# Ninety-one tiny loads as marks in a decode kernel that runs at the DMA engines' rate

## The chip, the cores and the metric

One core of a Trainium2 chip. The metric is device microseconds of one execution. SP, ACT and POOL below are the three engines that issue loads (SyncE, ScalarE, GpSimd); PE and DVE are the matmul and vector engines. "Landed" means that all of a load's semaphore increments have come. Each DMA engine has its own ring of work; a load "in the rings" has been issued and not yet moved. A mark is one of the tiny loads that the change adds, a series is fifteen of them, K8 is the K load of unit 8, and a drain is a stretch in which the rings hold no large load.

## The reference

One decode step of attention with a cached K and V, in sum with a gated MLP on the same normalised input:

```python
B, Sq, D = (4, 1, 640); H, Sk, Dh = (32, 4096, 128)
def _A_ref(x, k_cache, v_cache, wq, wo):
    q = (x @ wq).reshape(B, Sq, H, Dh)...            # cut
    scores = jnp.einsum('bhqd,bhkd->bhqk', q, k_cache) * Dh ** (-0.5)
    p = _softmax(scores, axis=-1)
    o = jnp.einsum('bhqk,bhkd->bhqd', p, v_cache)
    return (o ...) @ wo                              # cut
return x + _A_ref(xn, ...) + _B_ref(xn, ...)         # _B_ref: gMLP, weights of 3.3 MB in all
```

K and V together are 268 MB in bfloat16; every byte is read once.

## The kernel before

It cuts K and V into sixteen units each (8 heads of one batch entry, 8.4 MB) and streams them through five slots of one SBUF buffer. All large loads go over SP's queue, one unit ahead of the unit that is being worked on. The parts that the change touches:

```python
wq = at_slot(0, n_q)...; nc.sync.dma_start(out=wq, in_=A_wq...)          # 5.2 MB
nc.sync.dma_start(out=w_in, in_=B_w_in...)                               # 2.2 MB
nc.sync.dma_start(out=w_out, in_=B_w_out[0:nf, :]...)                    # 0.8 MB
for r in range(4):
    nc.sync.dma_start(out=w_rest[r:32:4], in_=w_rest_d[r])               # L125, 8 rows each
# ... cut: the order of units (k0 k1 k2 k3 v0 k4 v1 k5 ...) and their slots
def load_unit(item):
    # ... cut
    for t0, t1 in zip(c[:-1], c[1:]):
        nc.sync.dma_start(out=unit(item, t0, t1), in_=src[:, t0 * Dh:t1 * Dh])   # L161
def load_wo(g, c_cuts=(0, HG)):
    for c0, c1 in zip(c_cuts[:-1], c_cuts[1:]):
        nc.sync.dma_start(out=wo_t[g][:, c0:c1, :], in_=wo_q[g][:, c0:c1, :])    # L169
load_unit(seq[0])
# ... cut: constants on GpSimd, layer norm, q, the MLP
for i, item in enumerate(seq):
    if i + 1 < len(seq):
        key, u = seq[i + 1]
        # ... cut: x_res, the residual, 2 x 2.5 KB, ahead of the last V load but one
        load_unit(seq[i + 1])
        if key == "k" and u == 2 * B - 1:
            load_wo(u // B - 1)
    else:
        load_wo(NG - 3); load_wo(NG - 2); load_wo(NG - 1, (0, 4, 6, 7, 8))
    # ... cut: work on `item`
```

The framework that builds the program places every semaphore wait.

Of the kernel before, what the change touches and what calls it, by code (L numbers as in the profile page):

```python
# [12 lines left out]
BF16 = mybir.dt.bfloat16  # L13
# [3 lines left out]
def kernel(  # L17
# [19 lines left out]
    nc = tc.nc  # L37
    P = 128
    B, Sq, D = A_x.shape
# [27 lines left out]
    const = ctx.enter_context(tc.tile_pool(name="const", bufs=1))  # L67
# [78 lines left out]
    def unit(item, t0, t1):  # L146

        s0, s1 = place[item]
        assert s1 == s0 + 1 or t1 <= T // 2 or t0 >= T // 2
        if t0 >= T // 2:  # L150
            return at_slot(s1, (t1 - t0) * Dh, t0 * Dh - SL)
        return at_slot(s0, (t1 - t0) * Dh, t0 * Dh)

    def load_unit(item):
        key, u = item
        g, b = divmod(u, B)
        cache = A_k_cache if key == "k" else A_v_cache
        src = cache[b, g * HG:(g + 1) * HG].rearrange("e (m t) d -> (e m) (t d)", t=T)
        c = cuts.get(item, (0, T))
        for t0, t1 in zip(c[:-1], c[1:]):  # L160
            nc.sync.dma_start(out=unit(item, t0, t1), in_=src[:, t0 * Dh:t1 * Dh])  # L161
# [5 lines left out]
    def load_wo(g, c_cuts=(0, HG)):  # L167
        for c0, c1 in zip(c_cuts[:-1], c_cuts[1:]):
            nc.sync.dma_start(out=wo_t[g][:, c0:c1, :], in_=wo_q[g][:, c0:c1, :])  # L169

    load_unit(seq[0])


# [79 lines left out]
    MkH = SelH[:G]  # L253
    B32 = const.tile([G, B], BF16)
    nc.gpsimd.tensor_copy(out=B32[:], in_=Mk4[:G])

    NW = T // 4
    Zb = []
# [91 lines left out]
    def fill_qz(g):  # L350
        for hp in range(HP):
            r0 = 32 * hp
            nc.gpsimd.tensor_copy(out=QZ[r0:r0 + 32, :, :, :, 8 + 8 * hp],  # L353
                                  in_=qT[32 * g:32 * g + 32, NE * hp:NE * hp + NE].rearrange("p e a b -> p b a e"))
# [4 lines left out]
    def emit_K(u, k):  # L359

        g, b = divmod(u, B)
        hh = first.get(u, 0) ^ (k // 4)
        qp, kh = k // 2 % 2, k % 2
        t0 = 2 * TC * (2 * hh + qp)
        kw = unit(("k", u), t0, t0 + 2 * TC).bitcast(F32).rearrange("p (t w) -> p t w", w=KW)[:, :, 32 * kh:32 * kh + 32]
        kT = ktpool.tile([P, NKT], F32, tag="kT", name="kT")[:, 0:2 * TC * 32]
        nc.vector.transpose(kT[:].rearrange("p (t r) -> p t r", r=32), kw)  # L367
        if ("S", g) not in state:
            S_new = ps_s.tile([P, NE, TC, M], F32, tag="S", name="S")
            state[("S", g)] = S_new  # L370
        S_ps = state[("S", g)]
        kb = kT[:].bitcast(BF16).rearrange("p (i t e m w) -> p i t e m w", i=2, e=NE, m=M, w=2)
        w0 = 8 - (b * C2 + hh)
        for w in range(2):
            for e in range(NE):
                for i in range(2):
                    q = 2 * qp + i
                    nc.tensor.matmul(S_ps[32 * q:32 * q + 32, e], lhsT=QZ[:, b, 2 * kh + w, e, w0:w0 + 32],  # L378
                                     rhs=kb[:, i, :, e, :, w], start=(b == 0 and k < 4 and kh == 0 and w == 0),
                                     stop=(b == B - 1 and k >= 4 and kh == 1 and w == 1))  # L380
# [34 lines left out]
    def softmax(g):  # L415
        negmax = softmax_max(g)
        S_ps = state.pop(("S", g))
        p_bf = ppool.tile([P, TC, NE, M], BF16, tag="p", name="p")
        rowsum = small.tile([P, NE], F32, tag="rowsum")
        for e in range(NE):  # L420
            nc.scalar.activation(out=p_bf[:, :, e, :], in_=S_ps[:, e], func=ACT.Exp, bias=negmax[:, e:e + 1], scale=scale,  # L421
                                 accum_out=rowsum[:, e:e + 1])

        pT = ppool.tile([P, TC, HP, B * C2], BF16, tag="p", name="pT")
        nc.vector.transpose(pT[:].rearrange("p t h x -> p (t h x)"), p_bf[:].rearrange("p t e m -> p (t e m)"))  # L425

        xd = small.tile([P, B * C2, 4, TC], BF16, tag="xd", name="xd", bufs=1)
        state[("xd", g)] = xd
        for hp in range(HP):
            for q in range(4):  # L430
                op = nc.vector.tensor_copy if q < 2 or (hp < 3 and q == 2) else nc.scalar.copy
                op(out=xd[32 * hp:32 * hp + 32, :, q, :], in_=pT[32 * q:32 * q + 32, :, hp, :].rearrange("p t x -> p x t"))  # L432
        z_fill(g, 0)
        z_fill(g, 1)
        cs = misc_ps([G, 1], F32)
        for e in range(NE):
            nc.tensor.matmul(cs[:], lhsT=SelPe[:, e].rearrange("p h e b -> p (h e b)"), rhs=rowsum[:, e:e + 1],  # L437
                             start=(e == 0), stop=(e == NE - 1))
        rinv = small.tile([G, 1], F32, tag="rinv")
        nc.vector.reciprocal(out=rinv[:], in_=cs[:])  # L440
        state[("rinv", g)] = rinv
# [26 lines left out]
    def emit_sel(g):  # L468

        oh = misc_ps([G, Dh], F32)  # L470
        for b in range(B):
            nc.tensor.matmul(oh[:], lhsT=SelR[:, b].rearrange("p h b -> p (h b)"), rhs=state["R"][:, b, :],  # L472
                             start=(b == 0), stop=(b == B - 1))
        om = ppool.tile([G, HG, Dh], BF16, tag="p", name="om")
        nc.vector.scalar_tensor_tensor(out=om[:], in0=oh[:, None, :].to_broadcast((G, HG, Dh)),  # L475
                                       scalar=state.pop(("rinv", g))[:, 0:1],
                                       in1=MkH[:, :, None].to_broadcast((G, HG, Dh)), op0=ALU.mult, op1=ALU.mult)
        state[("om", g)] = om

    def emit_oT(g):  # L480
        om = state.pop(("om", g))[:].rearrange("p h (q c) -> p c h q", c=HG)
        oT_ps = misc_ps([P, HG, B], F32)
        for c in range(HG):
            nc.tensor.matmul(oT_ps[:, c, :], lhsT=om[:, c, :, :], rhs=B32[:], start=True, stop=True)
        oT = small.tile([P, HG + 1, B], BF16, tag="oT", bufs=3)
        nc.vector.tensor_copy(out=oT[:, 0:HG, :], in_=oT_ps[:])
        if g == NG - 1:
            nc.gpsimd.memset(oT[:, HG, :], 0.0)
        state[("oT", g)] = oT

    def emit_proj(g, cs=range(HG)):
        oT = state[("oT", g)]
        for c in cs:
            for hf in range(NH):
                r0 = 64 * (c % 2) + 32 * hf
                nc.tensor.matmul(proj[r0:r0 + B, 0:NO2], lhsT=oT[:, c, :],
                                 rhs=wo_t[g][:, c, hf * NO2:(hf + 1) * NO2],
                                 start=False, stop=(g == NG - 2 and c >= HG - 2))

    fill_qz(0)  # L500
# [3 lines that stand above are left out]
            if u == NU - 2 and key == "v":  # L504
                for hf in range(NH):
                    nc.sync.dma_start(out=x_res[32 * hf:32 * hf + B, :], in_=x_flat[:, hf * NO2:(hf + 1) * NO2])
            load_unit(seq[i + 1])
            if key == "k" and u == 2 * B - 1:
                load_wo(u // B - 1)
        else:  # L510
            load_wo(NG - 3)
            load_wo(NG - 2)
            load_wo(NG - 1, (0, 4, 6, 7, 8))
        key, u = item
        g, b = divmod(u, B)
        if key == "k":
            done = b == B - 1 and g > 0
            for k in range(8):
                emit_K(u, k)
                if done and k == 1:  # L520
                    emit_sel(g - 1)
                if done and k == 2:
                    emit_oT(g - 1)
                if done and k == 5 and g == 1:
                    emit_proj(g - 1)
            if b == B - 1:
                if g < NG - 1:
                    fill_qz(g + 1)
                softmax(g)
        else:  # L530
            emit_V(u)
# [59 lines left out]
```

## Time and profile before

| | before |
|---|---|
| median time | 664.23 us (2 runs, 664.21 to 664.24) |
| span in the profile | 662.5 us |
| bytes over the DMA engines | 282.61 MB, 427 GB/s on average |
| busiest compute engine | DVE, 54% |

How to read it: the compute engines have slack, the DMA engines have none. The prediction shows the lines; its first part explains them.

### The profile page before, as it was taken

The page shows a single profiled execution, that of the slowest core. Times are in us where ns is not written, and L with a number is a line of the kernel's source. Part 1 is how long each engine was busy: PE and PEld are TensorE (multiplying, and loading weights), DVE is VectorE, ACT ScalarE, POOL GpSimd, SP SyncE. Part 2 cuts the span into 40 slices and gives each one's busy share as a digit, 9 for nine tenths or more (in the row PEclk, how much of TensorE's full clock was granted, in tenths as well). Part 3 has the DMA queues.
Part 4 walks back from the last instruction along what each step waited for, and adds up shares of the span by engine and source line. Part 5 has one row for each costly group of instructions (what it writes and reads, how often), then busy time and mean ns, then how long its engine had stood idle before and what let it go on. Part 6 is the DMA issues. An engine that isn't in the chain of part 4 may idle for free.

```text
span 662.5 us, 5421 instructions
## 1 busy us (share of the span) xinstructions
PE 292.9 (44%) x2297; PEld 106.5 (16%) x2297; DVE 360.1 (54%) x275; ACT 78.4 (12%) x162; POOL 20.3 (3%) x64
## 2 busy tenths in 40 slices
PE   0636666256072556225336054533506254623245
PEld 0111122112021122111112022111202112211122
DVE  2249899556191759618256286745619185951112
ACT  0300000530100000530200000071010000053200
POOL 6210000000000000000000000000000000000000
PEclk9858768678577587677859596756958759667767
DMA  9999999999999999999999999999999999999996
GB/s 371 463 424 427 426 444 437 435 436 416 443 432 423 439 418 442 433 439 440 423 420 435 432 421 452 433 424 431 431 436 444 428 431 415 445 432 437 418 419 262
DMA packets 6901, 282.61 MB, mean 427 GB/s; under 512 B 808, under 2 KB 1084, under 8 KB 1468
## 3 DMA queue, kind: packets, MB, share of 16 engines
q1 hardware_dynamic: 6856, 282.25, 98.8%
q8 instruction: 18, 0.29, 0.2%
q14 instruction: 7, 0.06, 0.0%
q10 hardware_dynamic: 20, 0.01, 0.0%
HBM read 282.25 MB, written 0.01 MB: 426 GB/s over the span
## 4 chain that ended last, share of the span: by engine, by line
DMA 74%; DVE 11%; issue 11%; PE 2%; ACT 1%; SPq 0%; DVEq 0%; ACTq 0%
DMA kv<-in_A_k_cache_dram 64%; DVE kT L367 11%; DMA kv<-in_A_v_cache_dram 5%; DMA kv<-in_A_wo_dram 3%; DMA kv<-in_A_wq_dram 2%; PE O L449 2%; ACT xd L432 0%; ACT Zb L413 0%; ACT p L421 0%; DVE pT L425 0%; PE last_a L553 0%; DVE m L385 0%; PE S L378 0%; SPq L169 0%; PE misc L390 0%
## 5 line engine op out<-in xcount | busy, mean ns | idle before, releaser
L367 DVE STREAM_TRANSPOSE kT<-kv 128x2048 f32<-128x2048 f32 x128 | 282.8, 2276 | 124.7 <-DMA kv<-in_A_k_cache_dram 124.7
L378 PE MATMUL S<-kT,QZ 128*32 128x512 bf16 x1024 | 187.9, 500 | 230.6 <-DVE kT L367 230.6
L378 PEld LDWEIGHTS <-QZ 128*32 128x32 bf16 x1024 | 60.3, 111 | 353.4 <-issue 332.6
L449 PE MATMUL O<-kv,Zb 128*32 128x512 bf16 x1024 | 73.6, 451 | 58.2 <-DMA kv<-in_A_v_cache_dram 38.0
L458 DVE TENSOR_TENSOR om<-O,Mk 128x512 f32<-128x512 f32 x15 | 10.4, 692 | 109.0 <-PE O L449 109.0
L413 ACT ACTIVATE Zb<-xd,MkE 32x256 bf16<-32x256 bf16 x116 | 52.9, 498 | 110.4 <-PE O L449 109.0
L421 ACT ACTIVATE p<-S,negmax 128x512 bf16<-128x512 f32 x8 | 5.4, 683 | 400.6 <-DVE negmax L399 400.6
L449 PEld LDWEIGHTS <-Zb 128*32 128x32 bf16 x1024 | 32.9, 112 | 97.4 <-issue 55.8
L472 PE MATMUL misc<-R,SelR 128*32 128x128 f32 x32 | 6.4, 281 | 30.0 <-DVE R L459 28.4
L353 POOL COPY QZ<-qT 32x32 bf16<-32x32 bf16 x16 | 5.1, 318 | 390.6 <-PE S L378 389.9
L432 DVE COPY xd<-pT 32x256 bf16<-32x256 bf16 x44 | 16.0, 365 | 0.8
L459 DVE TENSOR_REDUCE R<-om 128x128 f32<-128x512 f32 x15 | 15.3, 1019 | 0.5
L432 ACT COPY xd<-pT 32x256 bf16<-32x256 bf16 x20 | 12.3, 614 | 5.6 <-DVE pT L425 5.2
L425 DVE STREAM_TRANSPOSE pT<-p 128x1024 bf16<-128x1024 bf16 x4 | 5.0, 1245 | 6.3 <-ACT p L421 6.3
L472 PEld LDWEIGHTS misc<-R,SelR 128*32 128x32 f32 x32 | 2.2, 107 | 37.8 <-DVE R L459 26.0
L385 DVE TENSOR_REDUCE m<-S 128x2 f32<-128x1024 f32 x4 | 4.9, 1225 | 5.5 <-PE S L378 5.5
L274 PE MATMUL q<-kv,xnT 128*32 128x512 bf16 x40 | 4.5, 630 | 6.9 <-DMA kv<-in_A_wq_dram 6.9
L461 DVE TENSOR_SCALAR R<-O,Mk 128x128 f32<-128x128 f32 x1 | 0.4, 351 | 12.5 <-PE O L449 12.5
L282 DVE CAST kv<-q 128x512 bf16<-128x512 f32 x1 | 0.7, 692 | 11.1 <-PE q L274 11.1
L390 PE MATMUL misc<-dg,ones_f 128*128 128x256 f32 x8 | 3.2, 488 | 7.6 <-DVE dg L387 7.6
L475 DVE SCALAR_TENSOR_TENSOR om<-misc,rinv,SelH 32x1024 bf16<-32x1024 f32 x4 | 5.1, 1271 | 2.0 <-PE misc L472 2.0
L437 PE MATMUL misc<-rowsum,SelPe 128*32 128x1 f32 x16 | 2.1, 202 | 9.0 <-ACT p L421 9.0
(102 smaller groups left out, 78.2 us busy)
## 6 DMA issues: line engine op xcount, KB each, us to landing
kv<-in_A_k_cache_dram SPq DMA_DIRECT2D x8, 4096.0 KB
kv<-in_A_v_cache_dram SPq DMA_DIRECT2D x1, 6144.0 KB
kv<-in_A_wq_dram SPq DMA_DIRECT2D x1, 5120.0 KB
kv<-in_A_wo_dram SPq DMA_DIRECT2D x3, 1280.0 KB
kv<-in_B_w_in_dram SPq DMA_DIRECT2D x1, 2160.0 KB, 19.9
kv<-in_A_v_cache_dram SPq DMA_DIRECT2D x1, 2048.0 KB
kv<-in_B_w_out_dram SPq DMA_DIRECT2D x1, 800.0 KB
kv<-in_A_wo_dram SPq DMA_DIRECT2D x1, 640.0 KB, 22.0
```

Of the source, the lines that this page charges most:

```text
L353: nc.gpsimd.tensor_copy(out=QZ[r0:r0 + 32, :, :, :, 8 + 8 * hp], in_=qT[32 * g:32 * g + 32, NE * hp:NE * hp + NE].rearrange("p e a b -> p ...
L367: nc.vector.transpose(kT[:].rearrange("p (t r) -> p t r", r=32), kw)
L378: nc.tensor.matmul(S_ps[32 * q:32 * q + 32, e], lhsT=QZ[:, b, 2 * kh + w, e, w0:w0 + 32], rhs=kb[:, i, :, e, :, w], start=(b == 0 and k < ...
L413: nc.scalar.activation(out=dst, in_=src, func=ACT.Copy, scale=mk)
L421: nc.scalar.activation(out=p_bf[:, :, e, :], in_=S_ps[:, e], func=ACT.Exp, bias=negmax[:, e:e + 1], scale=scale, accum_out=rowsum[:, e:e + 1])
L425: nc.vector.transpose(pT[:].rearrange("p t h x -> p (t h x)"), p_bf[:].rearrange("p t e m -> p (t e m)"))
L432: op(out=xd[32 * hp:32 * hp + 32, :, q, :], in_=pT[32 * q:32 * q + 32, :, hp, :].rearrange("p t x -> p x t"))
L449: nc.tensor.matmul(O_ps[32 * q:32 * q + 32, :, :], lhsT=Zb[b % 2][:, w].rearrange("p h c -> p (h c)"), rhs=vv[:, w * 4 * Dh:(w + 1) * 4 * ...
L458: nc.vector.tensor_tensor(out=om4[:], in0=O_ps[:], in1=Mk4[:, :, None].to_broadcast((P, 4, Dh)), op=ALU.mult)
L459: nc.vector.tensor_reduce(out=R, in_=om4[:].rearrange("p c d -> p d c"), axis=AX.X, op=ALU.add)
L472: nc.tensor.matmul(oh[:], lhsT=SelR[:, b].rearrange("p h b -> p (h b)"), rhs=state["R"][:, b, :], start=(b == 0), stop=(b == B - 1))
L475: nc.vector.scalar_tensor_tensor(out=om[:], in0=oh[:, None, :].to_broadcast((G, HG, Dh)), scalar=state.pop(("rinv", g))[:, 0:1], in1=MkH[: ...
```

## The change

Its intent is a tool for reading traces: loads of 1, 2, ... 15 rows are meant to run on as many DMA engines, so that their packets would show where each engine stands at five moments of the run. Nothing reads what they load.

```diff
+    mk = const.tile([16, 4, 136], BF16)
+    mk_ctr = [0]
+    def marks():
+        for k in range(1, 16):
+            nc.sync.dma_start(out=mk[0:k, mk_ctr[0] % 4, :], in_=A_wo[16 * k:17 * k, 0:136])
+            mk_ctr[0] += 1
+    marks()
     load_unit(seq[0])
@@ among the constants on GpSimd
+    mk2 = const.tile([1, 16, 64], BF16)
+    for k in range(16):
+        nc.gpsimd.dma_start(out=mk2[:, k, 0:31 + 2 * k], in_=A_wo[k:k + 1, 0:31 + 2 * k])
@@ main loop
             load_unit(seq[i + 1])
+            if key == "k" and u in (B, 2 * B, 3 * B):
+                marks()
             if key == "k" and u == 2 * B - 1:
                 load_wo(u // B - 1)
         else:
+            marks()
             load_wo(NG - 3)
```

## The prediction

> **What bounds the kernel now.** I read the page's busy shares first, then its slices, then the waits of the SP queue, then the chain that ended last, then single stretches of the timeline.
>
> ```profile
> span 662.5 us, 5421 instructions
> PE 292.9 (44%) x2297; PEld 106.5 (16%) x2297; DVE 360.1 (54%) x275; ACT 78.4 (12%) x162; POOL 20.3 (3%) x64
> ...
> DMA  9999999999999999999999999999999999999996
> ...
> DMA packets 6901, 282.61 MB, mean 427 GB/s; under 512 B 808, under 2 KB 1084, under 8 KB 1468
> ...
> DMA 74%; DVE 11%; issue 11%; PE 2%; ACT 1%; SPq 0%; DVEq 0%; ACTq 0%
> ```
>
> No compute engine passes 54%; the DMA digit is 9 in 39 of 40 slices and the chain is 74% DMA. The table of stretches shows the same at a finer grain: a DMA share of 1.00 and 430 to 433 GB/s from 24 to 650 us. So this kernel's time is its bytes over its rate, 282.6 MB at 427 GB/s = 662 us, and it holds only because the ring never runs dry. Any microsecond in which the slowest DMA engine has nothing queued is added to the end; nothing later can win it back.
>
> How far ahead is the queue filled? The timeline of SP and the chain around the K load that is unit 8 (the load after which the change puts its third series):
>
> ```profile
> 266.59 0.33 SPq L161 DMA_DIRECT2D kv<-in_A_k_cache_dram  x1
> 285.94 0.33 SPq L161 DMA_DIRECT2D kv<-in_A_v_cache_dram  x1
> 308.73 0.33 SPq L161 DMA_DIRECT2D kv<-in_A_k_cache_dram  x1
> ```
> ```profile
> 266.59 33.20 DMA kv<-in_A_k_cache_dram
> ```
>
> K8 is issued at 266.59 and has landed at 299.79. The V load behind it is issued at 285.94, 13.9 us before that, so it stands in the rings when K8 ends. SP itself is nearly always waiting, never working:
>
> ```profile
> SPq L161 <- DMA kv<-in_A_k_cache_dram: 182.1, 15, 19.6
> SPq L161 <- DVE kT L367: 155.9, 17, 16.8
> ...
> SPq L125 <- DMA kv<-in_A_wq_dram: 11.5, 1, 11.5
> ...
> SPq L586 <- DMA out_dram<-o_bf: 1.1, 1, 1.1
> ```
>
> The third line is the one to see. L125 loads the rest of w_out into its own buffer and shares no byte with wq, yet SP stood 11.5 us until wq had landed. The built program says why: loads of the hardware queues take eight semaphores in turn, and a load waits until the one eight before it, on its semaphore, has landed. It also shows waits of a load for an earlier load into the same bytes (K2, over K0's slot, waits for K0's semaphore as well as for K0's readers).
>
> **What the Trainium skill says.** "DMA: Bandwidth & Descriptors", section "Queues, rings and completion order": each DMA engine takes the descriptors of one ring in order. So a tiny load behind an 8 MB load on SP's queue lands only when that engine has done its share. The trace agrees: x_res, 2.5 KB, was issued at 581.33 and its four increments came between 607.58 and 610.72, beside the 606.25 to 610.62 of the V load ahead of it. The same page, "Why a DMA increments its semaphore by 16 and not by 1": a load of few rows runs on the lowest k engines, and one slow engine of the four came last here (610.72), so the slowest engine sits among the first four; a mark of 4 or more rows waits for it. "Perfetto Trace Analysis", section "DMA Instruction — HWDGE (DVE, Sync)": the profiled window of an issue leaves out the movement, so the 0.33 us above is SP's cost, not the load's. The DMA page's "Latency and other measured facts" has about 0.6 us to the first byte; here it was more: x issued at 0.73 has its first packet at 1.69, and the output issued at 660.00 at 0.82 us later. I use 0.9.
>
> **The change part by part.** Nothing is removed. In bytes it is nothing: 5 x 120 rows x 272 B = 163 KB and 16 rows of under 130 B, 0.4 us at 427 GB/s. In descriptors, 15 marks put at most 15 x 2 packets on one engine; a packet of 640 B took about 32 ns, so under 1 us on an engine in a series.
>
> The waits are the cost. The buffer has four slots and mark j+4 writes rows that mark j writes, so it waits for mark j to have landed, unread though it is; beyond this mark 8 waits for the load just ahead of the series (eight before it). SP is in order, so the next big load stands behind mark 15. For the series after K8:
>
> 1. Marks 1 to 4 are issued at once behind K8 and lie in the rings until K8's share on their engines is done, about 299.4 on the slowest engine.
> 2. Mark 1 lands 0.5 us later (own packet, its increment; increments follow their 4-byte packet by 0.35 to 0.45 us in this trace). SP has stood for 32 us by then, and the V load that had been issued at 285.94 has not been.
> 3. Marks 5 to 15 go out, eleven issues. By issue cost: x_res shows 0.37 us from one tiny issue to the next, the small wo pieces at the end 0.47; eleven are 4.1 to 5.2 us. By latency: a tiny load on an idle queue takes about 1.5 us from issue to landing (the output: 1.1 us of waiting after 0.4 us), so 5 to 8, 9 to 12 and 13 to 15 are two full rounds and three issues, 2 x 1.55 + 3 x 0.4 = 4.3. Both act together; I take 4.8.
> 4. The V load is issued and its first packet comes 0.9 us on.
>
> Sum: 0.5 + 4.8 + 0.9 = 6.2 us in which the slowest engine has nothing but marks. The faster engines end K8 up to 3.7 us earlier (its increments span 296.07 to 299.79) and idle longer, which costs nothing. Series 2 (after K4) and 4 (after K12) have the same form; K4's V load was issued only 7 us before K4 landed, but that is still ahead of it. So 3 x 6.2 = 18.6.
>
> The first series stands behind wq, w_in, w_out and the four w_rest loads and ahead of K0. In the kernel before, K0 is issued at 16.60, and the increments of the last w_rest come at 23.28 to 23.72, from where K0 flows. With marks, mark 3 waits for w_in (21.03), mark 4 for w_out (22.93), marks 5 to 8 for w_rest and for marks 1 to 4 (about 23.7): the rings empty, then the same eleven issues. K0 is issued at about 28.6 and flows from 29.5, 5.8 us late.
>
> The fifth stands behind the last V load, whose increments end at 649.67, and ahead of the six wo issues, which were all out at 637.2. They go out from 655 on; 9.7 us of wo and the same last products and output follow. 6.2 us.
>
> The sixteen loads on GpSimd's queue: POOL is done with its constants at about 14.6 and waits until 23.12 for the transposed q:
>
> ```profile
> 13.74 0.73 POOL L302 MEMSET kv<- 128x768 f32 x1
> 14.42 0.20 POOL L307 MEMSET one_bf<- 1x128 bf16 x1
> 23.12 0.29 POOL L285 COPY qT<-kv 128x128 bf16<-128x128 bf16 x1 [8.50 <-DVE kv L283]
> ```
>
> Each load costs POOL perhaps 1 us (the skill's figure for that path's start; no such load is in this trace), and the ninth may wait for the first. Some 16 to 20 us would bring q's copy from 23 to 31 to 35. What waits for it: the K1 load (needed in the ring when K0 ends, then about 49) and the query weights for the first product (needed at about 51). Hidden, 0 us.
>
> Sum: 5.8 + 18.6 + 6.2 = 30.6, less about 0.6 where series reset the engines' spread (all restart together): 30. Predicted 664.2 + 30 = 694.
>
> **The rivals.**
> - *Marks are only bytes.* If the waits for the four slots were not made, or the marks were sent ahead of the big loads, the change costs 0.4 to 2 us: 665 to 666. For it: the trace of before has spare time on SP (it waits 13.9 us ahead of need). Against it: the eight semaphores in turn alone make mark 8 wait for the load ahead of it and leave eight issues after that: 8 x 0.4 + 0.4 + 0.9 = 4.5 us a series, 687 in all. Also against: SP's order in the trace follows the program, even for x_res, which nothing held back.
> - *The first marks land on fast engines.* If marks 1 to 3 go to engines that end early, marks 5 to 7 are out before K8 is done and only mark 8 waits for all of it. Then eight issues remain, 4.5 us a series, 687. I give it a fifth.
> - *Issues on few engines are dear.* The w_rest loads of 8 rows took 0.62 us to issue, alone on the queue too (15.94). If marks cost this, eleven are 7.2 us and a series 8.6: 707.
> - *GpSimd becomes the bound.* If each of its loads cost 2.5 us or more, q's copy would come after 54, K1 would come late and the rings run dry once more, up to 10 us on top. The depth of 15 us speaks against.
> - *DVE or PE take over.* A series stops loads but no compute; DVE at 54% falls to about 52%. No.
>
> **Range and chances.** The issue cost (0.37 to 0.62) and whether mark 1 waits for the slowest engine set the spread: 687 at one end, 703 for somewhat dearer rounds (2.2 us of latency gives 7.1 a series, 698, and 0.5 us per issue adds to it). I say 686 to 703. Slower by over 2% means over 677.5; it takes 13.3 us, under half of the sum, so 0.95; within 2% 0.045.
>
> **What would show each step.** Right: five dips in the DMA row and in GB/s, near 24 to 30, 146, 311, 473 and past 660, each 5 to 7 us, GB/s outside them unchanged at 430 to 433; a stand of SP of some 30 us at the marks' line, waiting for a K load or for mk; in the timeline the V load that came 13.9 us before K8's end now about 5 us after it; wo issued after the last V has landed. POOL's copy of q after 30 with K1 still issued before K0 ends. Wrong: the V loads issued before the K load has landed (then no wait for slots), dips of 10 us (dearer issues), a sixth gap after K0 (GpSimd), or a lower rate between the dips, which none of these steps explains.

## The result, and the profile after

The changed kernel takes 671.81 us (2 runs, 671.29 to 672.32). The ratio to before is 1.0115, with a 95% interval of 1.0096 to 1.0134. (A ratio here and below is taken over the fast runs of the same rounds, so it isn't quite the ratio of the medians.) It is 7.6 us slower, where 30 had been predicted.

First the page of the changed kernel: its span, the GB/s of the 40 slices, the sum of DMA packets, and the chain by engine.

```profile
span 670.5 us, 5523 instructions
...
GB/s 373 381 428 423 411 434 444 434 435 428 439 435 422 430 417 456 415 431 431 434 436 431 431 412 453 438 435 438 412 439 423 431 430 423 442 431 434 433 403 192
DMA packets 8613, 282.78 MB, mean 422 GB/s; under 512 B 2520, under 2 KB 2796, under 8 KB 3180
...
DMA 76%; DVE 11%; issue 11%; PE 1%; SPq 1%; DVEq 0%
```

The bytes are up by 0.17 MB, as worked out (163 KB). But the GB/s row has none of the five dips that were predicted. There is a low second slice (381) and a low end (403, 192), and between them the rate of before. So the middle three series drained nothing. The timeline of SP around K8, whose times stand beside the three lines of before in the prediction, shows why (start us, duration us, engine, line, what; L176 is the marks' line):

```profile
269.88 0.33 SPq L161 DMA_DIRECT2D kv<-in_A_k_cache_dram  x1
270.27 1.18 SPq L176 DMA_DIRECT2D mk<-in_A_wo_dram  x4
289.25 0.35 SPq L161 DMA_DIRECT2D kv<-in_A_v_cache_dram  x1
301.90 1.88 SPq L176 DMA_DIRECT2D mk<-in_A_wo_dram  x4
312.10 0.35 SPq L161 DMA_DIRECT2D kv<-in_A_k_cache_dram  x1
322.74 1.41 SPq L176 DMA_DIRECT2D mk<-in_A_wo_dram  x4
326.26 0.35 SPq L161 DMA_DIRECT2D kv<-in_A_v_cache_dram  x1
```

The fifteen marks are not one block. After four of them comes the V load, at 289.25, which is 19.4 us after K8's issue, just as before (285.94 less 266.59). Marks 5 to 8 wait for marks 1 to 4 and are issued at 301.90, when the V load has long been in the rings. The order of SP's instructions in the two built programs says the same; this is the excerpt around K8, with the rows between marks 1 and 4 and so on cut:

```
 K load 128x32768
+mk 1x136 ... mk 4x136
 V load 128x32768
+mk 5x136 ... mk 8x136
 K load 128x32768
+mk 9x136 ... mk 12x136
 V load 128x32768
+mk 13x136 ... mk 15x136
```

The source says fifteen marks, then the V load. The builder laid down one big load after each four marks.

Where, then, do 7.6 us come from? From the two places where an interleaved load doesn't help. The start, SP's queue after and then before:

```profile
17.01 6.74 SPq L176 DMA_DIRECT2D mk<-in_A_wo_dram  x4
23.79 0.36 SPq L161 DMA_DIRECT2D kv<-in_A_k_cache_dram  x1
24.27 1.49 SPq L176 DMA_DIRECT2D mk<-in_A_wo_dram  x4
26.25 0.35 SPq L161 DMA_DIRECT2D kv<-in_A_k_cache_dram  x1
```
```profile
16.60 7.16 SPq L161 DMA_DIRECT2D kv<-in_A_k_cache_dram  x2
```

K0 is issued at 23.79 instead of 16.60. The stretches 20 to 26 and 26 to 32 us, before and after (the last two columns are the DMA share and GB/s):

```profile
20.00:26.00 6.00, 5.35 (x29) 1.07 (x24) 1.94 (x2) 0.69 (x2) 1.57 (x5) 1.00 1.22 520
26.00:32.00 6.00, 1.23 (x4) 0.59 (x3) 1.75 (x6) 4.35 (x6) 1.41 (x3) 0.68 0.98 426
```
```profile
20.00:26.00 6.00, 5.45 (x33) 1.20 (x25) 1.94 (x2) 0.59 (x1) 5.25 (x10) 1.00 1.02 349
26.00:32.00 6.00, 1.54 (x5) 0.59 (x3) 1.75 (x6) 4.14 (x6) 2.55 (x8) 0.66 0.81 350
```

(520 is more than sixteen engines do in steady flow, 433 at 27.1 GB/s each: packets are counted where they start.) Over these 12 us the rate is 350 instead of 473 GB/s, 1.48 MB less; at 427 GB/s that is 3.5 us.

And the end, before and then the changed kernel; before, all six wo loads went out from 631.59 to 637.2:

```profile
631.59 5.64 SPq L169 DMA_DIRECT2D kv<-in_A_wo_dram  x6
```
```profile
621.20 1.18 SPq L176 DMA_DIRECT2D mk<-in_A_wo_dram  x4
635.92 0.35 SPq L169 DMA_DIRECT2D kv<-in_A_wo_dram  x1
652.63 2.53 SPq L176 DMA_DIRECT2D mk<-in_A_wo_dram  x4
655.21 0.35 SPq L169 DMA_DIRECT2D kv<-in_A_wo_dram  x1
656.99 1.41 SPq L176 DMA_DIRECT2D mk<-in_A_wo_dram  x4
658.44 0.35 SPq L169 DMA_DIRECT2D kv<-in_A_wo_dram  x1
660.96 1.15 SPq L176 DMA_DIRECT2D mk<-in_A_wo_dram  x3
662.14 2.17 SPq L169 DMA_DIRECT2D kv<-in_A_wo_dram  x3
```

Here the load that slips ahead is a wo load of 1.3 MB, 3.1 us of DMA time (1.31 MB over 427 GB/s), and not a V load of 19.6 us. Each group of four marks waits for the group before, so the rings are fed one wo load at a time. The chain of the changed kernel runs through the marks at this point:

```profile
621.20 31.41 DMA mk<-in_A_wo_dram
...
652.63 4.34 DMA mk<-in_A_wo_dram
...
656.99 3.95 DMA mk<-in_A_wo_dram
```

### The profile page after: what moved, and what is told of

Same layout as the page of the kernel before. It is cut to its first block, busy times and chain, and to the rows that moved or that the text cites. A ratio compares the mean times of both kernels' runs of the same rounds, so it can differ in the third digit from the quotient of the medians.

```text
span 670.5 us, 5523 instructions
## 1 busy us (share of the span) xinstructions
PE 296.8 (44%) x2297; PEld 107.6 (16%) x2297; DVE 360.0 (54%) x275; ACT 78.4 (12%) x162; POOL 28.6 (4%) x80
## 4 chain that ended last, share of the span: by engine, by line
DMA 76%; DVE 11%; issue 11%; PE 1%; SPq 1%; DVEq 0%
DMA kv<-in_A_k_cache_dram 62%; DVE kT L380 11%; DMA mk<-in_A_wo_dram 6%; DMA kv<-in_A_v_cache_dram 4%; DMA kv<-in_B_w_out_dram 3%; PE O L462 1%; DMA kv<-in_A_wo_dram 0%; SPq L169 0%; SPq L176 0%; SPq L161 0%; DVE o_bf L576 0%; PE last_a L569 0%; DVEq L380 0%; SPq L113 0%; SPq L110 0%
## 5 line engine op out<-in xcount | busy, mean ns | idle before, releaser
L462 PE MATMUL O<-kv,Zb 128*32 128x512 bf16 x1024 | 76.1, 463 | 58.9 <-DMA kv<-in_A_v_cache_dram 38.8
L268 POOL DMA_DIRECT2D mk<-in_A_wo_dram x16 | 8.5, 537 | 3.7 <-DMA mk<-in_A_wo_dram 3.6
```

Source lines behind the costliest of these rows:

```text
L268: nc.gpsimd.dma_start(out=mk2[:, k, 0:31 + 2 * k], in_=A_wo[k:k + 1, 0:31 + 2 * k])
L462: nc.tensor.matmul(O_ps[32 * q:32 * q + 32, :, :], lhsT=Zb[b % 2][:, w].rearrange("p h c -> p (h c)"), rhs=vv[:, w * 4 * Dh:(w + 1) * 4 * ...
```

## The experiments

Twelve kernels ran, all correct, each with five rounds against the kernel before (the record of `e_in_order` holds four of its runs). The theory after the result (A): the builder interleaves the loads, so a series costs its packets only, except at the start, where marks and K0 wait for loads that are the last in the rings, and at the end, where the interleaved loads are short. Rivals: (B) the packets of the marks cost the same wherever they stand; (C) GpSimd's loads make the start late.

### One part at a time

`a_first`, `b_middle`, `c_last` keep one group of series and drop GpSimd's loads; `d_gpsimd` keeps those alone.

```diff
-    marks()                                            # dropped in b, c, d
-            if key == "k" and u in (B, 2 * B, 3 * B):  # dropped in a, c, d
-                marks()
-            marks()                                    # ahead of load_wo: dropped in a, b, d
-    for k in range(16):                                # GpSimd: dropped in a, b, c
+    for k in range(0):
```

> The first series of fifteen marks alone, no GpSimd loads. Theory A (the places count: K0 is issued at 23.8 instead of 16.6, after the rings have run empty): 3.5 to 4 us over before, near 668. Theory B (each mark costs its packets wherever it stands, 7.6 us over five series): 1.5 us, near 665.8. Theory C (the GpSimd loads make the start late): under 1 us, near 665.

> The three series in the middle alone. Theory A (the scheduler lets a K or V load go ahead after every four marks, so the rings never run dry): 0.3 to 1.2 us over before in all, 664.5 to 665.4. Theory B (packets, three fifths of 7.6): 4.5 us, near 668.8. The step of my prediction (three drains of 6.2): 683.

> The last series alone. Theory A (wo loads two to six stand behind marks that wait for the last V load, and only four marks and one wo load are in the rings at a time): 3 to 4 us over before, 667.2 to 668.2. Theory B: 1.5 us, 665.8. My prediction's step: 6.2 us, 670.4.

> The sixteen GpSimd loads alone. Theory A: 0 to 0.5 us over before, up to 664.7 (q's copy on POOL moves from 23.1 to about 26, K1 is still ahead of need). Theory C (they slow the start): 3 us or more, over 667.

| kernel | median us (5 runs) | over before (664.14, same rounds) | ratio, 95% interval |
|---|---|---|---|
| first series | 667.61 | 3.47 | 1.0054, 1.0041 to 1.0066 |
| three middle series | 665.03 | 0.89 | 1.0013, 1.0001 to 1.0026 |
| last series | 667.45 | 3.31 | 1.0050, 1.0037 to 1.0062 |
| GpSimd's sixteen | 664.60 | 0.46 | 1.0007, 0.9993 to 1.0020 |

The four sum to 8.1 us, at the upper end of the two runs of the whole change (7.1 to 8.1 over before). A holds in each, with the first series just under its 3.5; B misses all three kinds of series, and C, which had 3 us or more, is refused by 0.46. POOL does fall behind, but little. Its timeline in the run with its loads alone:

```profile
12.51 3.09 POOL L267 DMA_DIRECT2D mk<-in_A_wo_dram  x6
16.46 0.52 POOL L267 DMA_DIRECT2D mk<-in_A_wo_dram  x1 [0.86 <-DMA mk<-in_A_wo_dram]
...
26.14 0.28 POOL L297 COPY qT<-kv 128x128 bf16<-128x128 bf16 x1
```

A load costs POOL 0.52 us, the ninth does wait for the first (the bracket), and q's copy moves from 23.12 to 26.14, far ahead of the 43 us at which K0 lands.

What is the 0.3 us of a middle series (a third of 0.89, whose interval reaches from 0.1 to 1.7 us)? In the trace's packet records a row of 272 B took 19 ns and an increment 9 ns. If a load of k rows runs on the lowest k engines, as the prediction took it, fifteen marks put fifteen of each on the first engine, 0.42 us, and one of each on the fifteenth. That is the right size; it was not tested by a run of its own, and the packet records do not name their engine.

### The order that the prediction assumed

`e_in_order` ties every big load behind the last mark of the series ahead of it, with an edge that fixes the order of issue and adds no wait.

```diff
-            nc.sync.dma_start(out=mk[0:k, mk_ctr[0] % 4, :], in_=A_wo[16 * k:17 * k, 0:136])
+            last_mark[0] = nc.sync.dma_start(out=mk[0:k, ...], in_=...)
-            nc.sync.dma_start(out=unit(item, t0, t1), ...)     # the same for wo
+            behind_mark(nc.sync.dma_start(out=unit(item, t0, t1), ...))
```

> The whole change, with every big load tied behind the last mark of the series ahead of it (order of issue alone, no wait). This is the queue that my prediction assumed. If only the assumption about the order was wrong and the sum of a drain was right: 690 to 698, five dips of 5.5 to 7 us. If the waits of marks cost little even in this order (theory B, packets): 672, as the change itself.

698.56 us (4 runs, 697.83 to 698.88) against 664.22, ratio 1.0516 (1.0501 to 1.0530): 34.3 us slower. The five dips are there, 242, 259, 304, 258 and the end:

```profile
GB/s 373 242 422 466 429 394 449 421 259 471 421 421 426 432 435 454 423 380 304 470 430 421 426 419 460 434 418 258 474 426 422 422 425 416 461 433 425 420 316 228
```

SP's timeline around K8, and the stretches across the drain, in this run (the marks' line is L183 here):

```profile
281.78 0.33 SPq L168 DMA_DIRECT2D kv<-in_A_k_cache_dram  x1
282.16 35.27 SPq L183 DMA_DIRECT2D mk<-in_A_wo_dram  x15
317.48 0.39 SPq L168 DMA_DIRECT2D kv<-in_A_v_cache_dram  x1
```
```profile
306.00:312.00 6.00, 0.00 (x0) 0.00 (x0) 0.00 (x0) 0.00 (x0) 0.00 (x0) 0.50 0.93 404
312.00:318.00 6.00, 1.16 (x6) 0.48 (x7) 3.52 (x2) 0.00 (x0) 0.00 (x0) 0.50 0.04 8
318.00:324.00 6.00, 5.10 (x24) 1.53 (x23) 6.00 (x4) 0.00 (x0) 0.00 (x0) 0.50 1.00 383
```

Fifteen marks in one block, SP standing 35 us, a V load 35.7 us after K8's issue, and six microseconds at 8 GB/s. The packet records give the parts: K8's last packet ends at 313.98 and the V load's first starts at 318.50, 4.5 us in which the rings hold nothing but marks (4.5 at the drains after K4 and K12 too); then the first sixteen packets of 64 KB took 3.06 us on average where 2.42 is the rule. By the landings of the large loads, each against the same load of before, the stream falls back by 8.8 us at the first series, by 6.6, 5.7 and 5.7 at the middle ones, and at the last by 5.5 at the first wo load and 7.0 by the third. One step of the drain went another way than predicted: mark 5 was issued at 313.04, before K8's end, because mark 1 has one row and ran on one engine, which was not the last. The mark that held the rest was the eighth, at 314.47, which waits by its semaphore for all of K8. The excess of the first series, 8.8 against the 5.8 of the sum, can be read in part. Before, the first packets of K0 start at 21.59 to 23.38, not at the 23.7 from which the prediction counts; in this run they start at 30.13 to 30.82, not at 29.5, the two loads of x_res having come in among the marks; and they took 2.98 us on average. That leaves just under 1 us of the 3.0 unexplained.

### Fewer waits, and slower

`h_slots15` gives the buffer fifteen slots, so no mark of a series writes over another; rows are cut to 64 B to fit.

```diff
-    mk = const.tile([16, 4, 136], BF16)
+    mk = const.tile([16, 15, 32], BF16)
-            nc.sync.dma_start(out=mk[0:k, mk_ctr[0] % 4, :], in_=A_wo[16 * k:17 * k, 0:136])
+            nc.sync.dma_start(out=mk[0:k, mk_ctr[0] % 15, :], in_=A_wo[16 * k:17 * k, 0:32])
```

> The whole change with fifteen slots in the buffer instead of four (and rows of 64 B for want of room), so that no mark writes over another of its series. The built program then keeps the order of the source, all fifteen marks ahead of the next load, with the waits of the eight semaphores in turn alone: mark 8 waits for the load ahead. If those waits drain the rings: 4.2 to 5.1 us a series, 685 to 690, slower than the change though it waits for fewer things. If the waits for slots are the cost: 665 to 667.

696.79 us (696.41 to 696.87), ratio 1.0488 (1.0474 to 1.0503): 32.6 us slower than before and 25 us slower than the change, although its marks wait for less. The timeline around K8:

```profile
280.00 0.33 SPq L161 DMA_DIRECT2D kv<-in_A_k_cache_dram  x1
280.38 35.41 SPq L176 DMA_DIRECT2D mk<-in_A_wo_dram  x15
315.90 0.35 SPq L161 DMA_DIRECT2D kv<-in_A_v_cache_dram  x1
```

With fifteen slots the builder keeps the order of the source, and the eight semaphores in turn alone drain the rings. I had expected 685 to 690: the direction is right, the size too small. The slow first packets after a drain weren't in the sum, and the first series alone brings K0's landing from 43.38 to 51.03, 7.7 us. Taken with the kernel before it, this separates order from waits: with four slots a load was moved ahead and that saved the change; with fifteen none was. That the wait for a slot is what made the builder move it is an inference. The rows became shorter in the same edit. Two more programs were built and not run: four slots with rows of 64 B interleave just as the change does, so the row length is not the cause; eight slots, in which mark 9 still has to wait for mark 1, keep the order of the source, so a wait for a slot does not always move a load.

### The same loads in other places, and fewer of them

`f_moved` has all ninety-one loads, with the first series behind K0 and the last behind the V load of unit 11. (The builder then also puts the next loads between the groups of four.) `g_one` has one load of fifteen rows for each series.

```diff
-    marks()
     load_unit(seq[0])
+    marks()
-            if key == "k" and u in (B, 2 * B, 3 * B):
+            if (key == "k" and u in (B, 2 * B, 3 * B)) or (key == "v" and u == NU - 5):
-            marks()                                    # ahead of load_wo
```
```diff
-        for k in range(1, 16):
-            nc.sync.dma_start(out=mk[0:k, ...], in_=A_wo[16 * k:17 * k, 0:136])
+        nc.sync.dma_start(out=mk[0:15, mk_ctr[0] % 4, :], in_=A_wo[240:255, 0:136])
```

> The same ninety-one loads, the first series behind K0 instead of ahead of it and the last one behind the V load of unit 11 instead of behind the last V load. If the place makes the cost of the two dear series: 665.3 to 666.6 (0.3 a series and 0.5 for GpSimd's loads). If the number of marks makes it: 671 to 672.

> Each series one load of fifteen rows instead of fifteen loads, in the places of the change; GpSimd's loads as in the change. If waits among marks and the turn of the eight semaphores make the cost: 664.6 to 665.2. If a small load ahead of K0 and ahead of wo is dear by itself: 668 or more.

Moved: 666.47 us (666.25 to 666.92), 2.25 over before's 664.22, ratio 1.0035 (1.0022 to 1.0047). With 0.46 for GpSimd's loads, 1.8 are left for five series, 0.36 each, the price of a middle series. So the place made about 5.3 of the change's 7.6 us, and this is the version to use if the marks are wanted. One load a series: 664.54 us, 0.32 over before, ratio 1.0005 (0.9992 to 1.0018). The Trainium skill, "DMA: Bandwidth & Descriptors", section "Rules for kernel authors", says to coalesce many small transfers into one large one, because below 64 KB one pays mostly overhead. The advice holds here (0.3 against 7.6 us), but the overhead is not in the packets, at 19 ns each; it is in who waits for whom.

### Which marks of the dear series cost

`i_first2` and `j_first4` are the first series alone, cut to two and four marks; `k_last4` and `l_last8` the last series alone, cut to four and eight.

```diff
-        for k in range(1, 16):
+        for k in range(1, 3):      # i_first2; 5 in j_first4 and k_last4; 9 in l_last8
```

> The first series cut to two marks, nothing else. Neither waits for anything in flight; K0 falls on the semaphore of w_in and is issued at about 21.1. If the series is dear because marks 3 and 4 and then K0 wait for w_in, w_out and the first w_rest load until the rings are empty: 0 to 0.8 us over before, 664.1 to 664.9. If marks ahead of K0 are dear in themselves: two fifteenths of 3.5 us at least, with no way to tell.

> The first series cut to four marks. Marks 3 and 4 wait for w_in (21.0) and w_out (22.9), and K0 for a w_rest load, as in the whole series. If those waits are the cost: 2.8 to 3.6 us, 667.0 to 667.8, as the whole series, though eleven marks are gone. If marks 5 to 15 are: about 1 us, 665.1.

> The last series cut to four marks. None waits for a mark, and all six wo loads go out behind them. If the cost of the last series is the waits of marks 5 to 15 for marks behind the last V load: 0 to 0.4 us, 664.1 to 664.6. If marks ahead of wo are dear in themselves: a quarter of 3.3, 665.

> The last series cut to eight marks. Marks 5 to 8 wait for marks 1 to 4, behind the last V load, and wo two to six stand behind them; only the first wo load (1.3 MB, 3.1 us) is there to cover. One stall where the whole series has three: 1.0 to 2.5 us, 665.2 to 666.7. Packets alone: under 0.5 us.

| kernel | median us (5 runs) | over before (664.15) | ratio, 95% interval |
|---|---|---|---|
| first series, 2 marks | 665.93 (665.23 to 666.82) | 1.78 | 1.0025, 1.0013 to 1.0038 |
| first series, 4 marks | 667.46 | 3.31 | 1.0051, 1.0038 to 1.0064 |
| last series, 4 marks | 664.15 | 0.00 | 1.0000, 0.9987 to 1.0012 |
| last series, 8 marks | 665.85 | 1.70 | 1.0024, 1.0011 to 1.0038 |

Four marks cost the start what fifteen cost (3.31 and 3.47). Its stretch from 20 to 26 us is that of the whole change:

```profile
20.00:26.00 6.00, 5.35 (x33) 1.04 (x24) 1.94 (x2) 0.59 (x1) 1.58 (x5) 1.00 0.93 345
```

So it is marks 3 and 4, which wait for w_in and w_out by the turn of the semaphores, and K0 behind them. With two marks K0 itself takes w_in's semaphore and goes out at 21.14:

```profile
16.69 0.72 SPq L176 DMA_DIRECT2D mk<-in_A_wo_dram  x2
21.14 2.73 SPq L161 DMA_DIRECT2D kv<-in_A_k_cache_dram  x2
```

I had expected 0 to 0.8 us and got 1.78, with a wider scatter than any other kernel. Its first 64 KB packets start at 22.25 to 23.60, where before they start at 21.59 to 23.38, and they took 2.85 us on average where before each took 2.42: some engines had already run dry, and I had put no price on that. K0 lands 0.9 us later than before (44.32 against 43.38); where the other 0.8 us come from isn't shown. At the end, four marks cost nothing, since none waits for a mark, and eight cost one stall. Its SP timeline:

```profile
631.53 0.35 SPq L169 DMA_DIRECT2D kv<-in_A_wo_dram  x1
646.59 3.44 SPq L176 DMA_DIRECT2D mk<-in_A_wo_dram  x4
650.09 3.19 SPq L169 DMA_DIRECT2D kv<-in_A_wo_dram  x5
```

## Why the prediction was wrong

- **The bound** was right. The kernel loses what its DMA engines stand idle, and the end of the span doesn't win it back: with the first series alone K0 lands 3.6 us later than before (46.94 against 43.38), and the span is 4.0 us longer.
- **The step that failed** is the sentence "SP is in order, so the next big load stands behind mark 15", and with it the argument against the first rival, "SP's order in the trace follows the program, even for x_res, which nothing held back". A queue runs in the order in which it was laid down, but the builder laid it down otherwise than the source has it: after each four marks one big load. So the V load behind K8 went out 19.4 us after it, as before, and the three middle series cost 0.89 us in all; with the assumed order forced, the same loads cost 34.3 us. I took the source's order for the queue's, on the strength of one instruction. In the in-order run's program x_res itself has moved, in among the first series. By which rule the builder moves things I can't say in full. Seen in runs are three cases: four slots, interleaved; fifteen slots, not; an edge for order, not.
- **The sum of a drain** came out near once the order was forced, 34.3 us measured and 30.6 predicted, but in part by luck. Eleven issues from mark 5 to the V load took 4.4 us (313.04 to 317.48) against 4.8. The first packet came 1.0 us after the issue against 0.9. Mark 1 didn't wait for the slowest engine; the rival "the first marks land on fast engines" was right on that, as was its mark 8, and the rings stood empty of large loads for 4.5 us, which is that rival's figure and not the 6.2 of the sum. The slow first packets, about 0.65 us each time, stood in no sum and made up part of the difference; the middle series came to 6.6, 5.7 and 5.7. The first series exceeded its term by 3.0 us, in part because K0 had flowed from 21.59 and not from 23.7.
- **The three middle series** were given 18.6 us and cost 0.89. There the first rival, "marks are only bytes", was right, and I had refused it. The sum that I set against it, 687 us for the semaphores alone, was tested by `h_slots15`: 696.8 in the order of the source, so it was too low as well.
- **The first series** was given 5.8 and cost 3.47. The mechanism named (mark 3 waits for w_in, mark 4 for w_out) is the one that acts, as the run with four marks shows. The eleven issues that were to follow ahead of K0 didn't.
- **The last series** was given 6.2 and cost 3.31: one wo load went ahead of each group of four.
- **GpSimd's loads** were given 0 us, with q's copy at 31 to 35; it was at 25.9 in the change, and the cost was 0.46, not clear of zero in its interval. The 1 us a load that the prediction took from the DMA page's figure for that path's start was 0.52 us of POOL's time. Its rival, a start bound by GpSimd, was rightly refused.
- **Dear issues** (0.62 us) were rightly refused too: single marks took 0.24 to 0.43 us to issue. (The sum there is a little off: eleven issues of 0.62 us are 6.8 us, not 7.2, which makes 705 and not 707.)
- **The range** of 686 to 703 covered the kernel that I had described, not the one that was built. The chance of 0.045 for "within 2%" was the price of one unlooked-at assumption that every rival but the first shared.

Left open: the rule of the builder, just under 1 us of the in-order run's first series, 0.8 us of the first series with two marks, and a direct test of the 0.3 us of a middle series.

## What to carry to other kernels

Before arguing what a wait holds up, look at the order of the queue in the built program: the source's order is a request. Here marks that wait for less made the slower kernel (696.79 against 671.81 us), because the order of the queue changed with them. Fifteen tiny loads in a full queue cost 0.3 us here, about the size of their packets; what is dear is a tiny load that must wait for what is last in the rings, with the next large load behind it. If marks are wanted, put them behind a large load and not ahead of one, well before the tail.

## What the Trainium skill lacked or had wrong

- "DMA: Bandwidth & Descriptors" (Latency and other measured facts) has no price for a restart. After the rings had run empty, the first 64 KB packets of the sixteen engines took 2.6 to 3.8 us, against 2.42 in steady flow, on top of 0.8 to 1.1 us from issue to first packet (the page has about 0.6).
- The same page (Specifications) gives about 27 GiB/s per engine. A packet of 65,536 B took 2.42 us throughout, 27.1 GB/s, and sixteen engines make 433 GB/s; the figure fits as GB, not as GiB.
- The same page (Specifications) puts the smallest transfer for the full rate at 512 B. Below it the rate was lower, 272 B in 19 ns being 14.3 GB/s, and still fifteen such loads cost 0.3 us. No page that I read says that the waits of small loads can cost about twenty times that (5.7 us for a middle series in the order of the source).
- No page that I read says that the issue order of a queue can differ from the source's; here that was worth 27 us (698.56 against 671.81).
